# Two ways to form the shift of an exponent, beside a busy GpSimd

## The chip, the cores and the metric

The kernel runs on one core of a Trainium2 chip. The metric is the device time of one execution, in microseconds, and the median over the runs is compared. The core has TensorE (PE, with its weight loads PEld), VectorE (DVE), ScalarE (ACT), GpSimd (POOL) and SyncE (SP), which run their own instruction streams and meet at semaphores.

## The reference, cut to what matters

The work is an attention with random features, then a mixture of experts, then a second feed-forward network. Only the first part is touched:

```python
def phi(x):
    proj = np.einsum('bhsd,md->bhsm', x, omega)
    sq = np.sum(x * x, axis=-1, keepdims=True) / 2.0
    h = proj - sq
    h = h - np.max(h, axis=-1, keepdims=True)
    return np.exp(h) / np.sqrt(m)
q_p, k_p = (phi(q_s), phi(k_s))
kv = np.einsum('bhsm,bhsd->bhmd', k_p, v)
z = np.sum(k_p, axis=2)
num = np.einsum('bhsm,bhmd->bhsd', q_p, kv)
den = np.einsum('bhsm,bhm->bhs', q_p, z)[..., None] + 1e-06
return (num / den).astype(np.float32)
```

There are 4 batches, 8 heads, 576 tokens, 64 values to a head and 128 features. The exponent of a feature is proj + shift, where the shift of a token and head is -|x|²/2 - max h. Here |x|² is the sum of squares and max h is max proj - |x|²/2.

## The kernel before, in words

The 2304 tokens are 18 tiles of 128. A tile of keys (kp) or queries (qp) goes through these stages, each of them a method:

- `load` (L118) brings the tile with its features as rows of the array, and `load_rows` (L133) brings it with tokens on the partitions, both by SP's DMA queue.
- `squares` (L146) squares the tokens in place on GpSimd, a 128x512 product of two SBUF inputs.
- `sums` (L152) adds the squares of each head on VectorE, `ssq` of 128x8 (L157). It then issues the load of the rows two tiles on and the squares of the next tile.
- `colsplit` (L163) rounds the columns on ScalarE, and `colrest` (L173, the instruction at L181) subtracts, which gives the low part, `kpl` or `qpl`. Keys up to tile 6 do this on VectorE, all others on GpSimd.
- `proj` (L185) makes 24 products on TensorE into two PSUM banks, four heads to a bank. Most come from a ring of three banks, `pj`, so the second bank of one projection is free only when the exponentials of the projection before have read theirs.
- `most` (L204) takes the maximum over the features on VectorE, one reduction to a bank (L209), into `mx` of 128x8.
- `shift` (L211) makes `hm` = c·ssq + mx (L216) and `bias` = c·ssq - hm (L220), with c = -SCALE²/2. Both are VectorE operations with two 128x8 inputs in SBUF.
- `expo` (L223) makes eight exponentials on ScalarE, one to a head, with a column of `bias` each (L232).

`attention` (L397) writes the order by hand: one slot per tile, and each engine runs its instructions in the order in which the code issues them. First come five key tiles (L433). Slots 0 to 12 then work on a tile of keys, k = s + 5, and a tile of queries. In such a slot the order is: transposes of the last query features (`t_step`), shift of the last queries, sums of the keys, exponentials of the last queries, `t_rest`, sums of the queries, products of keys and values (`kv`), projection, maximum and shift of the keys, exponentials of the keys, `n_step` (outputs of queries two tiles back, L305, with five small VectorE operations), `x_step`, then projection and maximum of the queries. The shift of those queries comes at the start of the next slot. Slots 13 to 17 have queries alone; there the shift follows its maximum at once (L527).

`beside` (L842) puts work for the next stage between: in slots 8 to 15 GpSimd issues loads of expert weights (L574), in slots 10, 11, 12, 14 and 17 it subtracts a 128x1024 low part of such a weight (`lo_m`, L568), and in slots 14 to 17 a 128x288 part of the tokens (`xl_m`, L642). All these stand in GpSimd's one queue with the squares and the subtractions of `colrest`.

After the slots the two feed-forward networks run, products back to back on TensorE to the end.

The two operations of the shift:

```python
hm = self.qpool.tile([P, H], F32, tag="hm", name=f"hm_{tag}{t}", bufs=3)
nc.vector.scalar_tensor_tensor(hm, ssq, -0.5 * SCALE * SCALE, mx, op0=ALU.mult, op1=ALU.add)
if between:
    between()
bias = self.qpool.tile([P, H], F32, tag="bias", name=f"bias_{tag}{t}", bufs=3)
nc.vector.scalar_tensor_tensor(bias, ssq, -0.5 * SCALE * SCALE, hm, op0=ALU.mult, op1=ALU.subtract)
```

Of the kernel before, what the change touches and what calls it, by code (L numbers as in the profile page):

```python
# [7 lines left out]
F32 = mybir.dt.float32  # L8
# [29 lines left out]
def pieces(t):  # L38
    """(batch, first partition, last partition) of the tokens in tile t"""
    out, p = [], 0  # L40
    while p < P:
        b = (t * P + p) // S
        q = min(P, (b + 1) * S - t * P)
        out.append((b, p, q))
        p = q
    return out


class Kern:
# [5 lines left out]

# [1 line left out]
    def setup(self):  # L57
# [23 lines left out]

# [1 line left out]
    def bank(self, tag, name):  # L83
# [5 lines left out]
    def setup_attn(self):  # L89
        nc = self.nc  # L90
        self.cols, self.rows, self.vin, self.pj, self.bias = {}, {}, {}, {}, {}
        self.kv_ps = {}
        self.kp, self.qp, self.qpT, self.kv, self.xr = {}, {}, {}, {}, {}
        self.gpool = self.qpool
        self.lg = self.qpool.tile([P, NT, E], F32, name="lg")
        self.hl, self.ssq, self.mx = {}, {}, {}
        w = self.qpool.tile([P, 2 * M], F32, name="wom")
        nc.sync.dma_start(out=w, in_=self.a["wom"])
        nc.vector.tensor_scalar(w, w, SCALE, None, op0=ALU.mult)
        self.womh = self.qpool.tile([P, 2 * M], F32R, name="womh")  # L100
        self.woml = self.qpool.tile([P, 2 * M], F32R, name="woml")
        nc.vector.tensor_copy(self.womh, w)
        nc.vector.tensor_tensor(self.woml, w, self.womh.bitcast(F32), ALU.subtract)

    def gate_weights(self, wg):
        """two heads' at a time: block-diagonal w_gate"""
        nc = self.nc
        for j in range(2):
            nc.vector.tensor_copy(self.wg[j * D : (j + 1) * D, :, j, :], wg[j * D : (j + 1) * D])

    def warm(self):
        """products of no use, until the first tokens are here: the array's clock rises with use"""
        x = self.oneh.rearrange("p t e -> p (t e)")[:, 0:P]
        ps = self.bank("w0", "warm")
        for i in range(8):
            self.nc.tensor.matmul(ps[:, 0:P], x, x, start=True, stop=True)

    def load(self, tag, t):  # L118
        """one tile's tokens as columns, for the projection"""
        if t >= NT:  # L120
            return
        pool = self.kpool if tag == "kp" else self.qpool
        x = pool.tile([P, DM], F32, tag=tag + "c", name=f"{tag}c{t}", bufs=3 if tag == "kp" else 2)
        self.nc.sync.dma_start(out=x, in_=self.a["kk" if tag == "kp" else "qq"][t, :, 0, :])
        self.cols[tag, t] = x
# [26 lines left out]
    def sums(self, tag, t):  # L152
        if t >= NT:
            return
        sq = self.rows.pop((tag, t))
        ssq = self.ssq[tag, t] = self.qpool.tile([P, H], F32, tag="ssq", name=f"ssq_{tag}{t}", bufs=5)
        self.nc.vector.tensor_reduce(ssq, sq.rearrange("p (h d) -> p h d", h=H), axis=AX.X, op=ALU.add)  # L157
        if tag == "qp" or t > 5:
            self.load_rows(tag, t + 2)
        if tag == "qp" and t < 13 or tag == "kp" and t > 4:  # L160
            self.squares(tag, t + 1)
# [23 lines left out]
    def proj(self, tag, t):  # L185
        """two heads at a time: block-diagonal omega"""
        nc = self.nc
# [16 lines left out]
    def most(self, tag, t):  # L204
        """max over the features of x . omega"""
        mx = self.mx[tag, t] = self.qpool.tile([P, H], F32, tag="mx", name=f"mx_{tag}{t}", bufs=3)
        for i, ps in enumerate(self.pj[tag, t]):
            out = mx[:, 4 * i : 4 * i + 4]
            self.nc.vector.tensor_reduce(out, ps.rearrange("p (h m) -> p h m", h=4), axis=AX.X, op=ALU.max)  # L209

    def shift(self, tag, t, between=None):  # L211
        """- |x|^2 / 2 - max h, h = x . omega - |x|^2 / 2"""
        nc = self.nc
        ssq, mx = self.ssq.pop((tag, t)), self.mx.pop((tag, t))
        hm = self.qpool.tile([P, H], F32, tag="hm", name=f"hm_{tag}{t}", bufs=3)
        nc.vector.scalar_tensor_tensor(hm, ssq, -0.5 * SCALE * SCALE, mx, op0=ALU.mult, op1=ALU.add)  # L216
        if between:
            between()
        bias = self.qpool.tile([P, H], F32, tag="bias", name=f"bias_{tag}{t}", bufs=3)
        nc.vector.scalar_tensor_tensor(bias, ssq, -0.5 * SCALE * SCALE, hm, op0=ALU.mult, op1=ALU.subtract)  # L220
        self.bias[tag, t] = bias

    def expo(self, tag, t):  # L223
        """exp(h - max h)"""
        nc = self.nc
# [11 lines left out]
    def kv_part(self, b, t, i):  # L237
        """k'^T [v 1] of one tile and four heads, added to batch b's; the bank's first product clears the bank's flags"""
        nc = self.nc
# [22 lines left out]
    def kvg_turn(self, b):  # L262
        """k'^T v with its features first"""
        nc = self.nc
# [7 lines left out]
    def kvg(self, b):  # L272
        """k'^T v w_gate, head by head"""
        nc = self.nc
# [30 lines left out]
    def n_step(self, t):  # L305
        """tokens' outputs and the gate's logits, which are sums over the heads"""
        nc = self.nc
# [34 lines left out]

# [1 line left out]
    def gating(self, t0, t1):  # L344
# [16 lines left out]
    def gates(self, t0, t1):  # L361
        """the gate of a token's expert is 1 / sum of the exponentials; squared, as a later layer needs it"""
        nc = self.nc
# [9 lines left out]
    def counting(self, b):  # L373
        """tokens of each expert"""
        nc = self.nc
# [7 lines left out]
    def counted(self, b):  # L383
        """the fullest expert, and how many tokens are elsewhere"""
        nc, g, cn = self.nc, self.gpool, self.cnt[:, b, :]
# [11 lines left out]
    def attention(self, beside):  # L397
        """one slot per tile of tokens; every stage works on the tile one slot behind the stage before it"""
        nc = self.nc
        ends = {0: 0, 4: 1, 9: 2, 13: 3}  # L400

        def kv(s):
            """products of slot s: a tile's, and what the tile before has of the next batch"""
            t = s + 4
            for i in range(2):
                for tt, bb in [(t - 1, 1), (t, 0)]:
                    if 0 <= tt < NT and bb < len(pieces(tt)):
                        self.kv_part(pieces(tt)[bb][0], tt, i)
            if s in ends:
                self.kv_close(ends[s])  # L410
# [125 lines left out]
    def all_counted(self):  # L536
        """how many tokens of all are not with their batch's expert; what the general path reads"""
        nc = self.nc
# [4 lines left out]

# [1 line left out]
    def stage(self, name):  # L545
        return self.stg.tile([P, 2 * DM], F32, tag="st", name=name, bufs=4)

    def routed(self, b):
        """register with the expert that most tokens of batch b have"""
        self.expert[b] = self.nc.values_load(  # L550
# [7 lines left out]
    def split(self, pool, f, st, name, engines):  # L558
        """hi: 12 significant bits, lo: the rest; hi + lo is the float32 value"""
        nc = self.nc  # L560
# [31 lines left out]
    def narrow_load(self, c):  # L592
        """half a chunk of the FFN's float64 weights, as pairs of words"""
        f, i = divmod(c, 2)
# [4 lines left out]
    def narrow(self, c):  # L599
        """float64 -> float32: sign and top exponent bit, then 7 + 20 bits of the high word, then 3 of the low"""  # L600
        nc = self.nc
# [12 lines left out]

# [1 line left out]
    def steps(self):  # L616
# [10 lines left out]
    def xsplit(self, key, c):  # L627
        """hi and lo of 128 features of one half batch (or block)"""
        nc = self.nc
# [29 lines left out]
    def hidden(self, st):  # L659
        """relu (for the second FFN squared), hi and lo"""  # L660
        nc = self.nc
# [58 lines left out]
    def ffn_next(self):  # L720
        """first layer of the step after this one"""
        nxt = self.todo[self.at + 1] if self.at + 1 < len(self.todo) else None
# [15 lines left out]
    def extras(self, s):  # L738
        """weights made ready beside step s"""
        ev = self.events.get(s, [])  # L740
# [28 lines left out]

# [1 line left out]
    def general(self):  # L771
        """every expert over every token, masked, and the second FFN again; float32 products"""
        nc, tc = self.nc, self.tc
# [169 lines left out]
```

## Time and profile before

| what | us |
|---|---|
| median of 3 runs | 807.91 |
| the three runs | 807.91, 809.21, 801.22 |
| span of the profiled execution | 800.9 |

The page of the profile does not list a run time of the profiled execution beside its span. The span is what the trace covers from the first to the last instruction; it stands 0.3 us below the shortest of the runs and 7.0 us below their median.

How to read the rows further on: a row of a group of instructions ends with the time it was busy, the mean of one in ns, the idle time of its engine just before, and what ended that idle time. A row of a line (L157 and so on) gives the shortest, the median and the longest. A row of a timeline begins with the start and the length in us. [...]

### The profile page before, as it was taken

The numbers are of one execution on the slowest core, as the hardware profiler recorded it, in microseconds if no ns is written. First come the engines' busy times: TensorE is split into PE (matmuls) and PEld (weight loads), VectorE is DVE, ScalarE is ACT, GpSimd is POOL, SyncE is SP. The second block draws the span as 40 slices with busy tenths as digits, with TensorE's granted clock in tenths as the row PEclk, the third lists the DMA queues.
The fourth block names the chain that finished last, engine by engine and source line by source line (L and its number), as shares of the span: only waits on it lengthen the run. The fifth ranks groups of instructions, "written<-read, shape, count | busy, mean of one in ns | idle before, by whom it ended". The sixth has DMA issues, their size and how long they took to land.

```text
span 800.9 us, 12830 instructions
## 1 busy us (share of the span) xinstructions
PE 779.3 (97%) x4944; PEld 732.7 (91%) x4944; DVE 456.1 (57%) x900; ACT 332.7 (42%) x786; POOL 108.4 (14%) x114
## 2 busy tenths in 40 slices
PE   8999989889999999999999999999999999999997
PEld 7999978889999999999999999999999999999986
DVE  7888988896787788887874322322332232232222
ACT  4768657675433444334444322332232223233222
POOL 3546545561101001000000000000000000000000
PEclk9899989899999999999999999999999999999999
DMA  8746553362575666666660010010010001001001
GB/s 277 232 133 191 180 162 113 122 185 80 190 244 181 209 207 223 196 198 202 219 222 6 1 40 0 1 41 1 0 40 1 1 1 40 1 1 40 0 1 43
DMA packets 41603, 84.57 MB, mean 106 GB/s; under 512 B 4000, under 2 KB 13360, under 8 KB 41536
## 3 DMA queue, kind: packets, MB, share of 16 engines
q1 hardware_dynamic: 36864, 66.82, 25.6%
q0 software_dynamic: 4672, 16.86, 6.7%
q8 instruction: 41, 0.67, 0.3%
q14 instruction: 26, 0.21, 0.1%
HBM read 65.76 MB, written 17.91 MB: 104 GB/s over the span
## 4 chain that ended last, share of the span: by engine, by line
PE 86%; DVE 9%; ACT 1%; DMA 1%; issue 1%; POOL 0%; SPq 0%; ACTq 0%; POOLq 0%; DVEq 0%
PE y_f L702 25%; PE h_f L656 8%; PE h_f L655 8%; PE h_f L654 8%; PE y_m L692 4%; PE h_m L654 4%; PE h_m L655 4%; PE y_m L693 4%; PE y_m L694 4%; PE h_m L656 4%; PE n_ps L316 2%; PE kv_ps L245 2%; DVE bias_qp L220 2%; DVE mx_qp L209 1%; DVE hm_qp L216 1%; DVE mx_kp L209 1%
## 5 line engine op out<-in xcount | busy, mean ns | idle before, releaser
L675 DVE TENSOR_TENSOR r_f<-r_f,h_f 128x384 f32<-128x384 f32 x96 | 53.2, 554 | 255.1 <-ACT hh_f L674 255.1
L673 ACT ACTIVATE r_f<-h_f 128x384 f32<-128x384 f32 x96 | 47.1, 491 | 264.7 <-PE h_f L656 264.7
L702 PE MATMUL y_f<-hi_f,hh_f 128*128 128x512 f32 x288 | 113.6, 394 | 0.0
L702 PE MATMUL y_f<-lo_f,hh_f 128*128 128x512 f32 x288 | 113.5, 394 | 0.0
L702 PE MATMUL y_f<-hi_f,hl_f 128*128 128x512 f32 x288 | 113.3, 393 | 0.0
L669 ACT ACTIVATE hh_m<-h_m 128x288 fp32r<-128x288 f32 x64 | 26.4, 412 | 119.6 <-PE h_m L656 118.4
L654 PE MATMUL h_m<-xh_m,hi_m 128*128 128x288 f32 x256 | 75.8, 296 | 0.0
L692 PE MATMUL y_m<-hh_m,hi_m 128*128 128x288 f32 x256 | 75.6, 295 | 0.0
L655 PE MATMUL h_m<-xl_m,hi_m 128*128 128x288 f32 x256 | 75.4, 295 | 0.0
L694 PE MATMUL y_m<-hh_m,lo_m 128*128 128x288 f32 x256 | 75.4, 294 | 0.0
L693 PE MATMUL y_m<-hl_m,hi_m 128*128 128x288 f32 x256 | 75.4, 294 | 0.0
L656 PE MATMUL h_m<-xh_m,lo_m 128*128 128x288 f32 x256 | 75.4, 294 | 0.0
L702 PEld LDWEIGHTS y_f<-hi_f,hl_f 128*128 128x128 f32 x288 | 54.1, 188 | 12.4
L656 PE MATMUL h_f<-xh_f,lo_f 128*128 128x384 f32 x192 | 64.8, 337 | 0.0
L656 PE MATMUL h_f<-x_f,lo_f 128*128 128x384 f32 x192 | 64.8, 337 | 0.0
L655 PE MATMUL h_f<-xl_f,hi_f 128*128 128x384 f32 x192 | 64.7, 337 | 0.0
L655 PE MATMUL h_f<-x_f,hi_f 128*128 128x384 f32 x192 | 64.7, 337 | 0.0
L654 PE MATMUL h_f<-xh_f,hi_f 128*128 128x384 f32 x192 | 64.7, 337 | 0.0
L654 PE MATMUL h_f<-x_f,hi_f 128*128 128x384 f32 x192 | 64.6, 337 | 0.0
L702 PEld LDWEIGHTS y_f<-lo_f,hh_f 128*128 128x128 f32 x288 | 54.2, 188 | 8.8
L702 PEld LDWEIGHTS y_f<-hi_f,hh_f 128*128 128x128 f32 x288 | 54.0, 188 | 8.4
L676 DVE TENSOR_TENSOR hl_f<-r_f,hh_f 128x384 fp32r<-128x384 f32 x96 | 53.6, 559 | 10.4 <-PE y_f L702 0.5
(131 smaller groups left out, 1718.8 us busy)
## 6 DMA issues: line engine op xcount, KB each, us to landing
we<-we POOLq DMA_DIRECT2D x32, 512.0 KB, 5.1
wd<-wf SPq DMA_DIRECT2D x32, 512.0 KB, 5.3
wscr<-narrow SPq DMA_DIRECT2D x32, 256.0 KB, 2.1
wf<-wscr SPq DMA_DIRECT2D x16, 512.0 KB, 4.4
vin<-vv SPq DMA_DIRECT2D x18, 260.0 KB, 3.9
kpc<-kk SPq DMA_DIRECT2D x18, 256.0 KB, 3.5
kpr<-kk SPq DMA_DIRECT2D x18, 256.0 KB, 3.7
qpc<-qq SPq DMA_DIRECT2D x18, 256.0 KB, 3.0
```

The lines of the kernel that those rows point to most:

```text
L209: self.nc.vector.tensor_reduce(out, ps.rearrange("p (h m) -> p h m", h=4), axis=AX.X, op=ALU.max)
L654: nc.tensor.matmul(ps[:, :n], w1, xh[:, :n], start=(c == 0), stop=False)
L655: nc.tensor.matmul(ps[:, :n], w1, xl[:, :n], start=False, stop=False)
L656: nc.tensor.matmul(ps[:, :n], w2, xh[:, :n], start=False, stop=(c == KC - 1))
L669: nc.scalar.activation(hh[:, :n], ps, AF.Relu)
L673: nc.scalar.activation(r, ps, AF.Relu)
L675: nc.vector.tensor_tensor(r, r, ps, ALU.mult)
L676: nc.vector.tensor_tensor(hl, r, hh.bitcast(F32), ALU.subtract)
L692: nc.tensor.matmul(out, w1, hh[:, :HALF], start=(f == 0), stop=False)
L693: nc.tensor.matmul(out, w1, hl[:, :HALF], start=False, stop=False)
L694: nc.tensor.matmul(out, w2, hh[:, :HALF], start=False, stop=last)
L702: nc.tensor.matmul(acc[i], h[:, i * P : (i + 1) * P], w[:, DM:], start=(f == 0 and k == 0), stop=(last and k == 2))
```

## The change

The two-input operations of `shift` go. In their place a tile `three` of 128x8x3 holds, for each token and head, the maximum, -|x|²/2, and -max h. The first column is written by `most` itself. The second is written in `sums` by a new GpSimd operation, which scales `ssq` by c. `shift` then makes two reductions on VectorE: the negated sum of columns 0 and 1 into column 2, and the sum of columns 1 and 2 into `bias`. `ssq` has three buffers in place of five, and `three` has five. The argument `between`, which no caller used, goes too, and docstrings and comment lines are emptied, which makes no instruction.

```diff
     def sums(self, tag, t):
...
         sq = self.rows.pop((tag, t))
-        ssq = self.ssq[tag, t] = self.qpool.tile([P, H], F32, tag="ssq", name=f"ssq_{tag}{t}", bufs=5)
+        ssq = self.qpool.tile([P, H, 1], F32, tag="ssq", name=f"ssq_{tag}{t}", bufs=3)
         self.nc.vector.tensor_reduce(ssq, sq.rearrange("p (h d) -> p h d", h=H), axis=AX.X, op=ALU.add)
+        three = self.three[tag, t] = self.qpool.tile([P, H, 3], F32, tag="three", name=f"three_{tag}{t}", bufs=5)
+        self.nc.gpsimd.tensor_scalar(three[:, :, 1:2], ssq, -0.5 * SCALE * SCALE, None, op0=ALU.mult)
         if tag == "qp" or t > 5:
             self.load_rows(tag, t + 2)
         if tag == "qp" and t < 13 or tag == "kp" and t > 4:
...
     def most(self, tag, t):
-        """max over the features of x . omega"""
-        mx = self.mx[tag, t] = self.qpool.tile([P, H], F32, tag="mx", name=f"mx_{tag}{t}", bufs=3)
+
+        three = self.three[tag, t]
         for i, ps in enumerate(self.pj[tag, t]):
-            out = mx[:, 4 * i : 4 * i + 4]
+            out = three[:, 4 * i : 4 * i + 4, 0:1]
             self.nc.vector.tensor_reduce(out, ps.rearrange("p (h m) -> p h m", h=4), axis=AX.X, op=ALU.max)
 
-    def shift(self, tag, t, between=None):
-        """- |x|^2 / 2 - max h, h = x . omega - |x|^2 / 2"""
-        nc = self.nc
-        ssq, mx = self.ssq.pop((tag, t)), self.mx.pop((tag, t))
-        hm = self.qpool.tile([P, H], F32, tag="hm", name=f"hm_{tag}{t}", bufs=3)
-        nc.vector.scalar_tensor_tensor(hm, ssq, -0.5 * SCALE * SCALE, mx, op0=ALU.mult, op1=ALU.add)
-        if between:
-            between()
+    def shift(self, tag, t):
+
+        nc = self.nc
+        three = self.three.pop((tag, t))
+        nc.vector.tensor_reduce(three[:, :, 2:3], three[:, :, 0:2], axis=AX.X, op=ALU.add, negate=True)
         bias = self.qpool.tile([P, H], F32, tag="bias", name=f"bias_{tag}{t}", bufs=3)
-        nc.vector.scalar_tensor_tensor(bias, ssq, -0.5 * SCALE * SCALE, hm, op0=ALU.mult, op1=ALU.subtract)
+        nc.vector.tensor_reduce(bias, three[:, :, 1:3], axis=AX.X, op=ALU.add)
         self.bias[tag, t] = bias
```

## Rows read from the trace of the kernel before

**Rows 1.** The page: span, busy time of TensorE, and its granted clock in 40 slices.
```profile
span 800.9 us, 12830 instructions
...
PE 779.3 (97%) x4944; PEld 732.7 (91%) x4944; DVE 456.1 (57%) x900; ACT 332.7 (42%) x786; POOL 108.4 (14%) x114
...
PEclk9899989899999999999999999999999999999999
```

**Rows 2.** Windows by stretch: busy time of each engine, granted clock, DMA share, GB/s.
```profile
8.00:42.00 34.00, 32.89 (x228) 31.17 (x228) 30.46 (x57) 23.11 (x77) 18.11 (x16) 0.90 0.78 263
108.00:118.00 10.00, 9.28 (x52) 9.12 (x53) 8.12 (x18) 6.56 (x21) 3.50 (x4) 0.66 0.39 120
142.00:152.00 10.00, 8.31 (x45) 8.31 (x46) 7.27 (x22) 6.40 (x19) 3.36 (x5) 0.66 0.32 102
196.00:800.00 604.00, 599.12 (x3505) 560.39 (x3502) 292.38 (x541) 202.66 (x396) 13.82 (x26) 1.00 0.26 85
...
42.00:183.00 141.00, 128.10 (x1079) 122.63 (x1079) 123.32 (x265) 98.00 (x300) 73.95 (x66) 0.95 0.50 154
```

**Rows 3.** Waits in 42 to 183 us: who for whom, total, times, longest.
```profile
ACT qp L232 <- DVE bias_qp L220: 14.2, 7, 3.6
PE pj_kp L200 <- ACT qp L232: 7.0, 5, 2.6
PE pj_qp L200 <- ACT qp L232: 2.9, 3, 1.1
```

**Rows 4.** Timeline of 103 to 108 us, a slot with a long shift.
```profile
103.40 1.26 POOL L181 TENSOR_TENSOR qpl<-qpc,qph 128x512 fp32r<-128x512 f32 x1 [3.56 <-ACT qph L170]
103.62 1.07 DVE L216 SCALAR_TENSOR_TENSOR hm_qp<-ssq_qp,mx_qp 128x8 f32<-128x8 f32 x1
...
104.72 2.71 DVE L220 SCALAR_TENSOR_TENSOR bias_qp<-ssq_qp,hm_qp 128x8 f32<-128x8 f32 x1
...
105.35 1.05 POOL L150 TENSOR_TENSOR kpr<-kpr 128x512 f32<-128x512 f32 x1
...
106.36 1.04 POOL L150 TENSOR_TENSOR qpr<-qpr 128x512 f32<-128x512 f32 x1
...
107.52 0.62 ACT L232 ACTIVATE qp<-pj_qp,bias_qp 128x128 f32<-128x128 f32 x2 [3.55 <-DVE bias_qp L220]
```

**Rows 5.** Groups of 0 to 330 us: the four groups of the shift.
```profile
L220 DVE SCALAR_TENSOR_TENSOR bias_qp<-ssq_qp,hm_qp 128x8 f32<-128x8 f32 x18 | 16.4, 911 | 0.8
...
L216 DVE SCALAR_TENSOR_TENSOR hm_kp<-ssq_kp,mx_kp 128x8 f32<-128x8 f32 x18 | 10.9, 605 | 0.6
L216 DVE SCALAR_TENSOR_TENSOR hm_qp<-ssq_qp,mx_qp 128x8 f32<-128x8 f32 x18 | 10.7, 597 | 0.6
...
L220 DVE SCALAR_TENSOR_TENSOR bias_kp<-ssq_kp,hm_kp 128x8 f32<-128x8 f32 x18 | 4.8, 264 | 0.7
```

**Rows 6.** Lines L220, L157 and L350: shortest, median and longest in ns.
```profile
L220 DVE SCALAR_TENSOR_TENSOR bias_kp<-ssq_kp,hm_kp x18: 166/168/1117, 12.3 to 146.2; 128x8 f32<-128x8 f32 x18
...
L157 DVE TENSOR_REDUCE ssq_qp<-qpr x18: 669/675/678, 28.6 to 178.8; 128x8 f32<-128x512 f32 x18
...
L350 DVE TENSOR_REDUCE gmx<-lg x4: 177/184/188, 89.9 to 198.7; 128x5 f32<-128x40 f32 x2, 128x4 f32<-128x32 f32 x2
```

**Rows 7.** Window of 106 to 108 us, of the two-microsecond windows.
```profile
106.00:108.00 2.00, 0.13 (x2) 0.00 (x0) 2.00 (x3) 0.48 (x2) 1.40 (x2) 1.00 0.95 305
```

**Rows 8.** Groups on GpSimd, the first three in 42 to 183 us, the last over the span.
```profile
L568 POOL TENSOR_TENSOR lo_m<-we,hi_m 128x1024 fp32r<-128x1024 f32 x5 | 11.9, 2378 | 0.1
...
L574 POOL DMA_DIRECT2D we<-we x8 | 4.9, 607 | 0.0
L642 POOL TENSOR_TENSOR xl_m<-xT,xh_m 128x288 fp32r<-128x288 f32 x4 | 3.2, 790 | 2.4 <-ACT xh_m L640 2.4
...
L935 POOL MEMSET const-float32-0.0<- 128x1 f32 x1 | 0.1, 98 | 0.5 <-issue 0.5
```

**Rows 9.** Timeline of the start, 2 to 40 us: squares of key tile 1, shift of tile 0.
```profile
9.77 1.04 POOL L150 TENSOR_TENSOR kpr<-kpr 128x512 f32<-128x512 f32 x1 [2.65 <-DMA kpr<-kk]
...
11.28 1.00 DVE L216 SCALAR_TENSOR_TENSOR hm_kp<-ssq_kp,mx_kp 128x8 f32<-128x8 f32 x1
```

More of the change, by code (lines that the diff above doesn't have):

```diff
@@ L95, in setup_attn @@
         self.lg = self.qpool.tile([P, NT, E], F32, name="lg")
-        self.hl, self.ssq, self.mx = {}, {}, {}
+        self.hl, self.three = {}, {}
         w = self.qpool.tile([P, 2 * M], F32, name="wom")
```

## The prediction

> **What bounds the kernel now.** I read the page first. By its busy time TensorE works 97% of the 800.9 us, and its granted clock falls under 9 tenths in several of the first slices [rows 1]. So an average says little, and the second view is the windows by stretch. From 196 us to the end TensorE is busy 599.1 of 604 us at full clock with VectorE at 292.4, so nothing that VectorE saves there can count [rows 2]. The slots of the attention, 42 to 183 us, are another matter. Of these 141 us TensorE is idle for 141 - 128.1 = 12.9, and VectorE is busy for 123.3. [...]
>
> Third, the waits: in the slots TensorE stands for 7.0 us at the keys' projection and 2.9 us at the queries', both until the queries' exponentials have read a bank of the ring, and those exponentials stood 14.2 us for `bias` [rows 3]. So the chain there is: maximum, shift, exponentials, second bank of the next projection. Fourth, the timeline of one slot shows what the shift is made of. `hm` begins while GpSimd makes `qpl` and ends at 104.69, 0.03 us after `qpl` does at 104.66. `bias` ends at 107.43, 0.03 us after GpSimd's squares at 107.40. Two operations on 8 columns took 1.07 and 2.71 us, and ScalarE stood 3.55 us for them [rows 4]. The shortest `bias` took 0.166 us [rows 6]. So a two-input VectorE operation waits from inside for the GpSimd work beside it, to its end. In the window of 106 to 108 us TensorE is busy 0.13 of 2 us [rows 7], and the stretch that follows is the first of the two at 0.66 [rows 2].
>
> **What is removed.** 36 `hm` and 36 `bias`, 16.4 + 10.9 + 10.7 + 4.8 = 42.8 us of VectorE [rows 5]. At 0.166 each they would be 72 x 0.166 = 12.0 [rows 6]. The other 30.8 us are waiting.
>
> **What is added on VectorE.** 72 reductions of 16 values to 8. Does a reduction wait for GpSimd? The 18 of `ssq_qp` lie between 669 and 678 ns, and they too run beside squares and subtractions, so I say no; if it did, nothing would be saved (third rival). Their size: 512 values take 675 ns and 32 to 40 take 184, so (675 - 184)/(512 - 36) = 1.03 ns a value, and 16 values give 0.163 us [rows 6]. Below that they can't fall far, and above 0.184 they should not rise, as the larger ones take that. I take 0.17, or 12.2 us. VectorE saves 42.8 - 12.2 = 30.6 us. The maxima write with a stride of three words in place of one; I count that at nothing, with 0.1 us each as the bound, an estimate.
>
> [...] Were a small one as dear as the 512-value ones, 72 x 0.675 = 48.6 us would replace 42.8, and the time would be no better than before; the row of L350 shows that size sets the price [rows 6].
>
> **What is added on GpSimd.** 36 scalings of 8 columns. No such operation stands in the trace. From below it is a 128x1 fill, 0.098 us, from above the subtraction of 288 columns, 0.79 us [rows 8]. I take 0.2, nearer to the fill because the work is 8 columns: 7 us in all. GpSimd is busy 74.0 of the 141 us [rows 2], so the cover is 67 us, and even at 0.79 (28 us) it would hold in sum. What counts is where it stands. In `sums` it is issued ahead of the next squares and of all that GpSimd does after it: the squares, `kpl`, `qpl` and the loads of expert weights. So the squares now wait for VectorE's sum, which they did not. They are wanted a slot later, so that costs nothing unless a slot shrinks to GpSimd's own work. The load of the rows, issued by SP, stays where it was, and SP is not held, since GpSimd alone issues the scaling. `ssq` with three buffers is read by the scaling soon after; I see no wait there.
>
> **The new wait.** The shift waits for the scaling, and behind it on VectorE stand `bias`, the operations of `n_step` and the next maxima, and ScalarE's exponentials and TensorE's second bank wait for those. Whether the maxima, which write other columns of the same tile, wait too I can't see in this trace; if so the wait comes some 1.3 us earlier, as two maxima stand between. In most slots GpSimd finishes `qpl` (1.26 us) before or while VectorE sums the keys, then scales, and two more sums or copies and two maxima cover that. In slots 10, 11, 12, 14 and 17 `lo_m` (2.38 us) and an issue of a load (0.61 us) come between [rows 8]; there I expect up to 1 us of wait each, 5 us in all, and the bound from below is none. At the start the scaling of tile 0 stands behind the squares of tile 1, which end at 10.81, before `hm` began at 11.28 [rows 9], so nothing is lost if only the shift waits, and about 1 us if the maxima do.
>
> **The sum.** Not all of 30.6 us is on the path, because TensorE becomes the bound. It can win back its idle time, 12.9 us. I take three quarters, 9.7, and leave the rest to the slots with `lo_m` and to the latency of the chain. It can also win back the low clock: in each of the two stretches (1 - 0.66) x 10 = 3.4 us, so 6.8, as the idle time ahead of them goes. The low clock near the start, (1 - 0.90) x 34 = 3.4 us, I leave in, since little changes before it [rows 2]. So 9.7 + 6.8 = 16.5 us, and 800.9 - 16.5 = 784.4 by the profiled execution. That one lies 7.0 us under the median of the runs, 807.9. What the runs had more may be stalls and low clock of the same kind, which go, or something else, which stays. I take half: 784.4 + 3.5 = **788 us**.
>
> [...]
>
> **Rivals.** One: *TensorE is the bound already.* Half of its idle time goes, 6.5 us, and the low clock comes back after other gaps. That gives 800.9 - 6.5 = 794.4, and 798 with the same 3.5. For it speaks that TensorE is busy 128.1 of 141 us [rows 2]; against it that its waits are named, and 9.9 us of them hang on the queries' exponentials [rows 3].
>
> Two, on the other side: *GpSimd's queue sets the pace.* The maxima wait for the scaling, and the scaling for `qpl` or `lo_m`. Then the old wait stays in another place, and the two maxima, which ran before it, now run after it: some 1.36 us for each of the 18 key tiles, 24.5 us of VectorE. With about half on the path, as 16.5 of 30.6 above, that is +13, so 821 us. It decides from the point where the scaling ends more than 30.6/36 = 0.85 us, on the mean of all tiles, after the first maximum could start. For it speaks that GpSimd runs `qpl` just as the shift begins [rows 4], against it its 67 idle microseconds.
>
> Three: *the change doesn't do what it says.* The small reductions are held by GpSimd as the old operations were; then only the scalings are added, 809 us. Against it stand the even times of the sums [rows 6].
>
> **Chances.** Forecast 0.68, rival one 0.20, two 0.05, three 0.07. A difference of 1%, 8 us, is about what a measurement of this kernel can tell from no change; under 799.8 is faster. The forecast gives 0.66 faster and 0.02 same, rival one 0.14 and 0.06, rival three 0.06 same and 0.01 slower, rival two 0.05 slower: 0.80, 0.14, 0.06. The range: if all of TensorE's idle time and all three stretches of low clock go, 12.9 + 10.2 = 23.1 gives 777.8, and the gaps of the weight loads or all 30.6 us lie a little lower; I put 776. Upward it takes in rival one with 4 us to spare, 802.
>
> **What would show it.** Right: the 72 reductions lie near 0.17 us with no long one; ScalarE's wait for `bias` falls from 14.2 to under 4 us; no TensorE gap of over 2 us in the slots; the granted clock from 108 us on stays at 1.00; the first network begins some 16 us earlier and the rest is as long as before. Wrong: VectorE or ScalarE waits for GpSimd's scaling for more than 10 us in sum, TensorE's waits for the exponentials stay, or small reductions take over 0.5 us.

## The result, and the profile after

The changed kernel takes 780.8 us (median of four runs, 776.9 to 781.0) where the kernel before takes 804.9 on the same chip (median of four, 801.2 to 809.2): a ratio of 0.969, with a 95% interval of 0.9645 to 0.9736. That is 24.1 us less. The forecast was 788 from a median of 807.9, so 19.9 less; the median of before is 804.9 now because a fourth run took 801.8.

The page after: span, busy times, granted clock, and the line that opens the chain of work that ended last.

```profile
span 779.2 us, 12902 instructions
...
PE 767.3 (98%) x4944; PEld 723.4 (93%) x4944; DVE 429.4 (55%) x900; ACT 332.7 (43%) x786; POOL 118.3 (15%) x150
...
PEclk9999999999999999999999999999999999999999
...
PE 95%; DVE 2%; DMA 1%; ACT 0%; SPq 0%; issue 0%; POOL 0%; DVEq 0%
```

Against [rows 1] the span falls by 21.7 us and VectorE by 26.7, and GpSimd gains 9.9. In the chain VectorE is now 2%; it was 9% before, with TensorE at 86%.

Where did the 21.7 go? I cut both traces at two products that both have: the key-value product behind the transpose of the keys of the slots (41.61 us before, 38.20 after) and the first product of the first network (181.85 and 160.56). The rest of the span is as long as it was, 619.0 and 618.6 us. So 3.4 us were gained ahead of the slots, 17.9 in them and 0.4 behind. The slots of before by this cut, in the view of [rows 2]:

```profile
41.61:181.85 140.24, 127.34 (x1075) 121.87 (x1073) 122.59 (x263) 97.08 (x296) 73.19 (x66) 0.95 0.50 155
```

And after, with a stretch of low clock and the two networks:

```profile
38.20:160.56 122.36, 119.60 (x1075) 116.52 (x1073) 100.38 (x264) 97.21 (x296) 81.60 (x94) 0.99 0.56 177
...
108.00:112.00 4.00, 4.00 (x24) 4.00 (x22) 1.64 (x4) 0.00 (x0) 2.23 (x2) 0.57 0.67 243
...
175.00:779.00 604.00, 598.81 (x3502) 560.08 (x3500) 292.04 (x541) 202.75 (x396) 13.85 (x26) 1.00 0.26 85
```

Read the first number (the length) less the second (TensorE busy): 12.9 us idle before, 2.8 after, so 10.1 won. The clock (the third figure from the end, a fraction of full speed): the two stretches of 10 us at 0.66 in [rows 2] lost 3.4 each, so 6.8 before; after, the stretch of 4 us at 0.57 loses 1.7, so about 5.1 won. These make 15.2 of the 17.9. Read the third number, the weight loads, in place of the second and the gaps are 18.4 before and 5.8 after, 12.5 won, and 12.5 + 5.1 = 17.6. The records of the products overlap: from 105.38 to 105.85 us of before they start 0.12 us apart and are listed with 0.28 each, where the weight loads are listed with 0.19. So a gap of up to 0.16 us between two products would not show, and of up to 0.07 between two weight loads.

The groups that answer to [rows 5], with the scalings that are new:

```profile
L159 POOL TENSOR_SCALAR three_kp<-ssq_kp 128x8 f32<-128x8 f32 x18 | 5.7, 316 | 8.0 <-DVE ssq_kp L157 7.0
L159 POOL TENSOR_SCALAR three_qp<-ssq_qp 128x8 f32<-128x8 f32 x18 | 4.2, 234 | 2.8 <-DVE ssq_qp L157 1.4
...
L219 DVE TENSOR_REDUCE bias_kp<-three_kp 128x8 f32<-128x16 f32 x18 | 3.1, 170 | 0.7
L219 DVE TENSOR_REDUCE bias_qp<-three_qp 128x8 f32<-128x16 f32 x18 | 3.1, 170 | 0.8
...
L217 DVE TENSOR_REDUCE three_kp<-three_kp 128x8 f32<-128x16 f32 x18 | 3.1, 170 | 2.0
L217 DVE TENSOR_REDUCE three_qp<-three_qp 128x8 f32<-128x16 f32 x18 | 3.1, 170 | 1.8
```

Four times 3.1 is 12.4 us in place of 42.8, with no long one: the longest of these 72 takes 0.172. The slot that answers to [rows 4] shows why that helps:

```profile
95.86 1.27 POOL L183 TENSOR_TENSOR qpl<-qpc,qph 128x512 fp32r<-128x512 f32 x1 [2.80 <-ACT qph L172]
...
96.46 0.17 DVE L217 TENSOR_REDUCE three_qp<-three_qp 128x8 f32<-128x16 f32 x1
...
96.67 0.17 DVE L219 TENSOR_REDUCE bias_qp<-three_qp 128x8 f32<-128x16 f32 x1
...
96.93 2.18 ACT L231 ACTIVATE qp<-pj_qp,bias_qp 128x128 f32<-128x128 f32 x8 [0.19 <-DVE bias_qp L219]
```

Both reductions run while GpSimd makes `qpl`, which ends at 97.13; before, `hm` ended 0.03 us behind that subtraction and `bias` 0.03 us behind the squares. That slot was no exception: of the 72 operations of before, 31 take over 0.25 us, and each of the 31 ends 0.02 to 0.03 us behind an instruction of GpSimd. What they take above 0.168 us each comes to 30.7 us, which is all of the waiting. ScalarE stood 0.19 us for `bias` here, and 3.55 there. The waits of 42 to 165 us:

```profile
ACT kp L231 <- DVE bias_kp L219: 12.9, 7, 4.8
...
PE t_ps L295 <- DVE lgh L326: 2.5, 2, 1.6
...
ACT qp L231 <- DVE bias_qp L219: 1.5, 5, 0.7
...
PEld pj_qp L202 <- ACT kp L231: 0.4, 2, 0.2
...
PEld pj_qp L202 <- ACT qp L231: 0.2, 1, 0.2
```

And two lines of the waits of before, 42 to 183 us, beside those of [rows 3]:

```profile
ACT kp L232 <- DVE bias_kp L220: 5.5, 3, 2.1
...
PE pj_qp L200 <- ACT kp L232: 2.1, 4, 0.7
```

ScalarE's wait for the queries' `bias` has gone from 14.2 to 1.5, but its wait for the keys' has risen from 5.5 to 12.9, so the sum fell only from 19.7 to 14.4. What counts is what reaches TensorE. Its products stood 9.9 us for the queries' exponentials and 2.1 for the keys'; none of these waits is left at its products, and 0.2 and 0.4 at its weight loads.

### The profile page after: what moved, and what is told of

It is laid out like the page before. It is cut to its first block, busy times and chain, and to the rows that moved or that the text cites. A ratio compares the mean times of both kernels' runs of the same rounds, so it can differ in the third digit from the quotient of the medians.

```text
span 779.2 us, 12902 instructions
## 1 busy us (share of the span) xinstructions
PE 767.3 (98%) x4944; PEld 723.4 (93%) x4944; DVE 429.4 (55%) x900; ACT 332.7 (43%) x786; POOL 118.3 (15%) x150
## 4 chain that ended last, share of the span: by engine, by line
PE 95%; DVE 2%; DMA 1%; ACT 0%; SPq 0%; issue 0%; POOL 0%; DVEq 0%
PE y_f L701 26%; PE h_f L655 9%; PE h_f L654 9%; PE h_f L653 9%; PE kv_ps L244 5%; PE y_m L691 4%; PE h_m L653 4%; PE h_m L654 4%; PE y_m L693 4%; PE y_m L692 4%; PE h_m L655 4%; PE n_ps L315 3%; PE t_ps L295 2%; PE pj_qp L202 1%; PE pj_kp L202 1%; PE pj_qp L203 1%
## 5 line engine op out<-in xcount | busy, mean ns | idle before, releaser
L701 PEld LDWEIGHTS y_f<-hi_f,hl_f 128*128 128x128 f32 x288 | 54.1, 188 | 12.4
```

Source lines behind the costliest of these rows:

```text
L701: nc.tensor.matmul(acc[i], h[:, i * P : (i + 1) * P], w[:, DM:], start=(f == 0 and k == 0), stop=(last and k == 2))
```

## The experiments

Each ratio is against the kernel before on the same chip, whose medians were 801.5 to 802.5. My theory: a VectorE operation that reads two tiles of SBUF waits from inside for GpSimd's work beside it and a reduction doesn't, and this wait, not the count or size of the operations, is what the change took away.

**The same tile, but two-input operations.**

```diff
-nc.vector.tensor_reduce(three[:, :, 2:3], three[:, :, 0:2], axis=AX.X, op=ALU.add, negate=True)
+nc.vector.tensor_tensor(three[:, :, 2], three[:, :, 0], three[:, :, 1], ALU.add)
-nc.vector.tensor_reduce(bias, three[:, :, 1:3], axis=AX.X, op=ALU.add)
+nc.vector.tensor_tensor(bias, three[:, :, 1], three[:, :, 2], ALU.subtract)
```

> The changed kernel with everything kept (tile of three columns, scaling on GpSimd, three buffers of ssq), but the two reductions of the shift made again by two-input operations on the same columns. Theory (waiting): a VectorE operation with two SBUF inputs waits for the GpSimd operation beside it, a reduction does not, and this is all of the gain. Then the time goes back near that of before, 800 us (794 to 806), and the two operations take over 0.5 us in the mean. Rival (layout): the gain comes from the scaling being off VectorE, the tile of three or the buffers. Then the time stays at 781 us (778 to 784) and the operations at 0.17 us.

Measured: 801.9 us, ratio 1.000 (0.997 to 1.003). The groups, same stretch as [rows 5]:

```profile
L217 DVE TENSOR_TENSOR three_qp<-three_qp 128x8 f32<-128x8 f32 x18 | 12.7, 707 | 1.8
L219 DVE TENSOR_TENSOR bias_qp<-three_qp 128x8 f32<-128x8 f32 x18 | 11.0, 610 | 0.8
L219 DVE TENSOR_TENSOR bias_kp<-three_kp 128x8 f32<-128x8 f32 x18 | 9.9, 551 | 0.7
...
L217 DVE TENSOR_TENSOR three_kp<-three_kp 128x8 f32<-128x8 f32 x18 | 6.1, 340 | 3.0 <-POOL three_kp L159 1.3
```

They sum to 39.7 us where before has 42.8, and the whole gain is gone, with the scaling on GpSimd, the tile of three columns and the order of the change all kept. The kind of operation is the cause; the rest of the change by itself moves nothing that can be measured.

**Only the second operation two-input.**

```diff
-nc.vector.tensor_reduce(bias, three[:, :, 1:3], axis=AX.X, op=ALU.add)
+nc.vector.tensor_tensor(bias, three[:, :, 1], three[:, :, 2], ALU.add)
```

> The changed kernel with only the second operation of the shift made by two inputs, the first stays a reduction. Theory (waiting): the second now stands where the first stood and waits for the same GpSimd work, so nearly all of the waiting comes back in one operation: its mean is over 0.9 us, time 796 us (789 to 802). Rival (each operation pays its own wait): about half of the loss, mean of the second near 0.6 us, time 787 to 791.

Measured: 789.4 us, ratio 0.986 (0.980 to 0.991).

```profile
L219 DVE TENSOR_TENSOR bias_qp<-three_qp 128x8 f32<-128x8 f32 x18 | 14.1, 783 | 0.8
L219 DVE TENSOR_TENSOR bias_kp<-three_kp 128x8 f32<-128x8 f32 x18 | 6.8, 380 | 0.7
```

The time lies in both ranges, so the means decide. I had thought that the second operation would take over the wait that the first no longer makes, with over 0.9 us in the mean, and that theory falls: it takes 0.58, and in sum 14.1 + 6.8 = 20.9 us, as with both two-input, 11.0 + 9.9 = 20.9. That the two sums are equal is partly chance, as the queries pay 3.1 us more and the keys 3.1 less. The rival held: each operation pays for what GpSimd runs beside it, and each that is replaced gives its own share back, here some 12 us of the 21 to 24 of the whole change.

**Before, without the squares.** The squares on GpSimd are left out, so the sums add the values themselves; half of the sum cancels in the exponent.

```diff
 def squares(self, tag, t):
...
-        self.nc.gpsimd.tensor_tensor(x, x, x, ALU.mult)
+        pass
```

> The kernel before without the squares on GpSimd: its sums add the tokens' values and not their squares. Theory (waiting): bias of the queries waited mostly for the squares, so its mean of 911 ns falls under 350 ns, while hm, which waits for the subtractions of colrest and of the expert weights, keeps 450 to 700 ns; time 790 us (784 to 797). Rival (the long operations come from their own semaphores or from VectorE): means as before and time within 3 us of before.

Measured: 794.2 us, ratio 0.991 (0.989 to 0.994).

```profile
L216 DVE SCALAR_TENSOR_TENSOR hm_qp<-ssq_qp,mx_qp 128x8 f32<-128x8 f32 x18 | 13.5, 749 | 0.6
L216 DVE SCALAR_TENSOR_TENSOR hm_kp<-ssq_kp,mx_kp 128x8 f32<-128x8 f32 x18 | 8.6, 478 | 0.6
L220 DVE SCALAR_TENSOR_TENSOR bias_qp<-ssq_qp,hm_qp 128x8 f32<-128x8 f32 x18 | 7.2, 398 | 0.8
...
L220 DVE SCALAR_TENSOR_TENSOR bias_kp<-ssq_kp,hm_kp 128x8 f32<-128x8 f32 x18 | 3.0, 167 | 0.7
```

This is the same cause from the other side: with VectorE's code untouched, less work on GpSimd makes `bias` of the queries fall from 911 to 398 ns. I expected under 350 there and 790 us. The time came 7.6 us under the 801.8 of before. What stayed is `hm` of the queries, which rose from 597 to 749, above what I expected: `qpl` and the low parts of the weights still run beside it, and all 21 operations that still take over 0.25 us end 0.02 to 0.03 us behind `kpl`, `qpl` or a low part. The squares carry 42.8 - 32.3 = 10.5 us of the waiting, a third.

**Scaling on VectorE.** Does an operation with one input wait too?

```diff
-self.nc.gpsimd.tensor_scalar(three[:, :, 1:2], ssq, -0.5 * SCALE * SCALE, None, op0=ALU.mult)
+self.nc.vector.tensor_scalar(three[:, :, 1:2], ssq, -0.5 * SCALE * SCALE, None, op0=ALU.mult)
```

> The changed kernel with the scaling of the sums on VectorE instead of GpSimd; it has one input, of 8 columns in SBUF. Theory (only two SBUF inputs wait): the 36 scalings take some 0.17 us each, 6 us of VectorE that has room, and the time stays at 781 us (777 to 784). Rival (any VectorE operation of this kind may wait for GpSimd): their mean is over 0.4 us, and the time 786 to 795 us.

Measured: 785.4 us, ratio 0.982 (0.973 to 0.991). The groups, and one slot's timeline:

```profile
L159 DVE TENSOR_SCALAR three_qp<-ssq_qp 128x8 f32<-128x8 f32 x18 | 11.0, 613 | 0.6
...
L159 DVE TENSOR_SCALAR three_kp<-ssq_kp 128x8 f32<-128x8 f32 x18 | 8.6, 476 | 0.6
```

```profile
56.43 1.27 POOL L183 TENSOR_TENSOR qpl<-qpc,qph 128x512 fp32r<-128x512 f32 x1 [3.55 <-ACT qph L172]
...
57.12 0.61 DVE L159 TENSOR_SCALAR three_kp<-ssq_kp 128x8 f32<-128x8 f32 x1
...
58.66 1.04 POOL L150 TENSOR_TENSOR qpr<-qpr 128x512 f32<-128x512 f32 x1
...
58.95 0.78 DVE L159 TENSOR_SCALAR three_qp<-ssq_qp 128x8 f32<-128x8 f32 x1
```

The time lies between the two ranges, and the means, 0.61 and 0.48 us, are the rival's. My theory in its narrow form ("only two inputs wait") falls. The scaling ends at 57.73, 0.03 us behind `qpl` at 57.70, and at 59.73, 0.03 behind the squares at 59.70. Its shortest takes 0.172 us, its longest 2.640; 36 x 0.172 = 6.2 of the 19.6 us are work. Of the three kinds tried here only the reductions stay at their size, 0.170 us in the mean and 0.172 at the longest. So the scaling's place on GpSimd is a part of the gain, by the medians some 5 of the 21 to 24 us; the intervals of the ratios overlap, so that size is rough. Why the reductions don't wait no run shows.

**The scaling later.** It is put behind the next tile's squares and a product of no use on GpSimd, to find what the new wait costs.

```diff
-        self.nc.gpsimd.tensor_scalar(three[:, :, 1:2], ssq, -0.5 * SCALE * SCALE, None, op0=ALU.mult)
...
             self.squares(tag, t + 1)
+        junk = self.qpool.tile([P, 320], F32, tag="junk", name=f"junk_{tag}{t}", bufs=1)
+        self.nc.gpsimd.tensor_tensor(junk, sq[:, 0:320], sq[:, 0:320], ALU.mult)
+        self.nc.gpsimd.tensor_scalar(three[:, :, 1:2], ssq, -0.5 * SCALE * SCALE, None, op0=ALU.mult)
```

> The changed kernel with the scaling put behind the squares of the next tile on GpSimd, and behind a product of 320 columns into a tile that nothing reads: the scaling comes some 1.9 us later, and GpSimd has 28 us more work. In the profile of the changed kernel the scaling of a key tile ends 2.6 us ahead of the shift that reads it (56.19 and 58.82 us in one slot). Theory (GpSimd's queue has that much to spare): 781 to 785 us, VectorE's wait for the scaling under 6 us in sum. Rival (GpSimd's queue is the next limit): the waits come to over 15 us and the time to 788 us or more.

Measured: 784.1 us, ratio 0.977 (0.970 to 0.983).

```profile
DVE three_kp L219 <- POOL three_kp L165: 4.8, 4, 1.7
...
DVE three_qp L219 <- POOL three_qp L165: 1.7, 3, 0.7
```

Delayed by some 1.8 us a tile (the squares' 1.04 and 0.75 of the product), the scaling holds VectorE for 6.5 us in seven places, a little over the 6 that I expected at most, and the run takes 3 us more, in which the product's own weight on GpSimd is not told apart. The waiting line is the shift (L219 here), never the maxima (L213), though these write columns of the same tile. That answers what the prediction left open, and with it goes its second rival.

**Only the maxima.** The half square stands in h and in max h, and cancels. So the rows' loads, squares, sums, scalings and both reductions are left out, and the maximum is written with its sign turned, as `bias`.

```diff
-            out = three[:, 4 * i : 4 * i + 4, 0:1]
-            self.nc.vector.tensor_reduce(out, ps.rearrange("p (h m) -> p h m", h=4), axis=AX.X, op=ALU.max)
+            out = bias[:, 4 * i : 4 * i + 4]
+            self.nc.vector.tensor_reduce(out, ps.rearrange("p (h m) -> p h m", h=4), axis=AX.X, op=ALU.max, negate=True)
```

> The changed kernel with bias taken as the negated maximum alone (the half square cancels in exact arithmetic): the rows' loads, squares, sums, scalings and the two small reductions are left out, some 36 us of VectorE and 48 us of GpSimd. Theory (after the change TensorE is the bound in the slots): little is left to win, its 2.8 us of gaps and some of the start: 773 us (769 to 778). Rival (VectorE or GpSimd still sets the pace): half of VectorE's 36 us comes off, 763 us or less.

Measured: 770.8 us, ratio 0.962 (0.956 to 0.967). The slots of its profiled run, and two stretches of low clock:

```profile
36.00:153.00 117.00, 117.00 (x1039) 115.30 (x1038) 72.52 (x177) 94.82 (x291) 47.57 (x40) 0.96 0.43 132
...
30.00:36.00 6.00, 6.00 (x41) 5.93 (x39) 1.56 (x3) 2.40 (x8) 1.65 (x2) 0.72 0.43 132
...
102.00:114.00 12.00, 12.00 (x65) 11.93 (x65) 4.07 (x9) 5.10 (x13) 2.70 (x3) 0.57 0.18 61
```

The profiled run is the slowest of the five, 776.9 us; the other four take 769.8 to 771.7, with a mean clock of 0.995 to 0.998 where this one has 0.989, so they can't hold all of this low clock. TensorE is never idle in the slots, while VectorE is busy 72.5 of 117 us, against 100.4 of 122.4 in the changed kernel. So without any shift TensorE is the bound there, and all that leads to the shift costs the changed kernel 7 to 10 us still (it takes 24.1 us less than before on its chip, this run 31.1 less on its own). And the clock falls here with TensorE busy all of the time.

**Full rows.** Those stretches begin inside runs of 32 products over 64 of the 128 rows, for the two tiles which two batches share. Here these products run over all 128 (the sums then hold the other batch's tokens too).

```diff
-                self.kp[t][lo:hi, 4 * i + j, :],
-                self.vin[t][lo:hi, 4 * i + j, :],
+                self.kp[t][:, 4 * i + j, :],
+                self.vin[t][:, 4 * i + j, :],
```

> The changed kernel with the products of keys and values of the two tiles that two batches share made over all 128 rows instead of 64 (the other batch's tokens are added too). The number of products and their columns stay. Theory (the low clock that is left comes with the 64-row products, since both stretches begin inside or right behind a run of them, with TensorE busy): the granted clock stays at 1.00 from 20 us on, and the time falls by the 3 to 4 us of the two stretches, 777 us (774 to 779). Rival (it comes from something else): both stretches stay, 781 us.

Measured: 777.3 us, ratio 0.969 (0.962 to 0.975). Stretches of the changed kernel, then the same ones here:

```profile
26.00:38.00 12.00, 12.00 (x86) 11.45 (x86) 7.70 (x19) 8.51 (x30) 9.02 (x12) 0.86 0.64 204
...
100.00:116.00 16.00, 16.00 (x124) 15.63 (x124) 10.09 (x27) 10.41 (x32) 8.07 (x10) 0.89 0.52 177
```

```profile
26.00:38.00 12.00, 11.49 (x102) 11.29 (x102) 9.71 (x23) 10.39 (x35) 10.01 (x14) 1.00 0.62 216
100.00:116.00 16.00, 15.90 (x141) 15.70 (x141) 11.40 (x28) 12.96 (x39) 9.80 (x11) 1.00 0.51 169
```

Both low stretches are gone, and 3.5 us with them. Three of its four runs have a mean clock of 0.998, one 0.994. But that the 64 rows are the cause isn't shown. The run with only the second operation two-input makes the 64-row products as the changed kernel does (32 of them from 30.19 and from 106.87 us), and its clock stays up:

```profile
30.00:40.00 10.00, 9.74 (x83) 9.19 (x81) 7.75 (x17) 9.32 (x32) 7.73 (x10) 1.00 0.60 193
108.00:116.00 8.00, 8.00 (x69) 7.86 (x70) 4.36 (x12) 4.36 (x17) 4.75 (x7) 1.00 0.60 190
```

Nine kept traces have two such runs of 32 each, and a low stretch begins inside ten of the 18; of the four runs over full rows, two here and two in the next kernel, none has one. And the changed kernel's own fastest execution, 776.9 us at a mean clock of 0.998, is as fast as the fastest here. So 3.5 us is what the low clock costs; what brings it is suggested only.

**Both together.** Only the maxima, and for the shared tiles a value tile with zeros at the other batch's tokens, so that products over 128 rows give the same sums.

```diff
+        if len(pieces(t)) > 1:
+            for b, lo, hi in pieces(t):
+                v = self.vin[t, b] = self.kpool.tile([P, H, VW], F32, tag=f"vs{lo}", name=f"vin{t}_{b}", bufs=1)
+                rest = slice(hi, P) if lo == 0 else slice(0, lo)
+                self.nc.gpsimd.memset(v[rest], 0.0)
+                self.nc.sync.dma_start(out=v[lo:hi], in_=self.a["vv"][t][lo:hi])
+            return
...
-                self.kp[t][lo:hi, 4 * i + j, :],
-                self.vin[t][lo:hi, 4 * i + j, :],
+                self.kp[t][:, 4 * i + j, :],
+                self.vin[t, b][:, 4 * i + j, :],
```

> Two findings together: bias is the negated maximum alone, as in the run with only the maximum, and the products of the two shared tiles run over 128 rows, with the other batch's tokens of the value tile filled with zeros. In the slots of the run with only the maximum TensorE has no gaps, and what is left is two stretches of low clock, 2 to 3 us and 5 us. Theory (the low clock comes with the 64-row products): both go, 766 us (763 to 769). Rival: they stay or come elsewhere, 771 us.

Measured: 768.8 us (768.5 to 768.9), ratio 0.959 (0.956 to 0.963), with a mean clock of 0.998 or 0.999 in each run. It beats both kernels, by 4.1% and by 1.5%, and lies at the upper end of the range.

```profile
36.00:151.00 115.00, 115.00 (x1069) 113.93 (x1069) 75.70 (x184) 97.25 (x294) 51.83 (x44) 1.00 0.45 137
```

**The changed kernel once more**, beside it on the same chip.

> The changed kernel as it is, on the same chip as the run before it, for the distance between the two: 781 us (777 to 784), with or without one of the two stretches of low clock, by which its runs differ by about 4 us.

Measured: 780.4 us, ratio 0.973 (0.969 to 0.977): the first result again. One stretch of its profiled run:

```profile
122.00:136.00 14.00, 12.46 (x88) 12.09 (x87) 10.04 (x31) 8.74 (x25) 6.64 (x8) 0.76 0.29 94
```

Here the low clock follows 1.5 us in which TensorE stood idle, and 108 to 112 us, right behind its 64-row products, is at 1.00. So the clock falls behind idle time too, and not at these products in every run.

## Why the prediction was right, and where its terms were not

- **The cause and the saving on VectorE**: right. 30.4 us saved, 30.6 worked out; 170 ns a reduction, as taken; a maximum takes 0.683 to 0.688 us after and took 0.683 to 0.684 before, so its new stride costs nothing. The two-input and squares runs show the cause from both engines. Nor is a small reduction as dear as one of 512 values, the case in which the prediction saw no gain: 0.170 us stands beside the 0.166 of the shortest `bias` [rows 6].
- **The scalings**: 0.2 us taken, 0.316 (keys) and 0.234 (queries) measured, 9.9 us for 7. They lie beside other work and cost nothing that shows.
- **The new wait**: up to 5 us expected in five slots, none measured; it comes only when the scaling is delayed by some 1.8 us.
- **ScalarE's wait**: the sign "under 4 us" holds for the queries' `bias`, 1.5, and not with the keys', 14.4 in sum. The prediction counted the queries' alone. Two other signs held: the longest gap of TensorE in the slots is 1.64 us, and the first network begins 21.3 us earlier.
- **TensorE's idle time**: the step was too small. Three quarters of 12.9 gave 9.7; 10.1 went by that measure and 12.5 by the weight loads. With the second figure the account of the slots closes to 0.3 us. The gaps of the weight loads, which the range names, were 141 - 122.6 = 18.4 us [rows 2]. With three quarters of them, 13.8, the sum would have been 780.3 for a span of 779.2, in place of 784.4; that it comes so near is luck, as the start, which neither sum has, makes up for 13.8 and 6.8 being too large.
- **The low clock**: 6.8 expected back, about 5.1 came. The step "as the idle time ahead of them goes" holds for 142 to 152 us in the first profile; in the repeat a stretch came back behind idle time. At 108 us TensorE was busy throughout and the clock fell all the same: the sign "at 1.00 from 108 us on" was wrong. It fell at the end of the 64-row products, and that these are the cause is not shown.
- **The start**: the largest miss. Nothing expected, 3.4 us measured. At 7.3 us a projection product of before took 0.41 us, one of after 0.28, but the lead is lost again as TensorE then stands 1.45 us for `kpl` of VectorE: the first product that reads tile 1's `kpl` starts at 11.41 before and 11.21 after. By 28 us the lead is 1.9. VectorE, for which the products wait there, has lost 0.8 at `hm` of tile 0 (1.00 us for 0.17, [rows 9]) and 0.8 at a copy of the gate's weights which stood beside squares (two copies in 1.21 us, in 0.36 after). The last 1.5 us is a shorter stretch of low clock, (33.61 x 0.10) - (30.20 x 0.06).
- **The 3.5 us added to the median**: wrong. The runs of after lie within 4.1 us of each other, those of before within 8.0. Of the 7.0 us between span and median 1.7 was no difference between executions at all: each run whose span is listed stands 1.5 to 2.0 us above it, so after with 780.9 for 779.2. What the slower runs of before had more went too.
- **The rivals**: TensorE as the bound is near where the change ends, not where it began; GpSimd's queue and held reductions are excluded by the waits and the groups above.

## What to carry to other kernels

Where a VectorE operation of a few columns takes anything from its floor to several times that, compare its end with the ends of GpSimd's instructions: 0.02 to 0.03 us behind one of them, as with 31 of the 72 operations here, is a wait that no view lists. Here a reduction over a small tile took it off, with 0.170 us in the mean for 0.264 to 0.911, and so did the scaling's place on the other engine, with 0.316 and 0.234 us for 0.476 and 0.613. Then cut both traces at the same two instructions and count TensorE's gaps by its weight loads as well as by its products.

## What was not expected of the hardware

The wait goes both ways. At the start four of GpSimd's scalings meet a subtraction of VectorE that came first and take 0.56 to 0.65 us in place of 0.23, as this one, which ends 0.14 behind that subtraction at 15.13:

```profile
14.45 0.68 DVE L183 TENSOR_TENSOR kpl<-kpc,kph 128x512 fp32r<-128x512 f32 x1
...
14.62 0.65 POOL L159 TENSOR_SCALAR three_kp<-ssq_kp 128x8 f32<-128x8 f32 x1 [0.80 <-DVE ssq_kp L157]
```

And it moves on to what is left. VectorE's busy time fell by 26.7 us and not by 30.4, since other two-input operations now meet GpSimd more than before: of the gating, `gsh` takes 1.6 us more in sum and `gfi` 1.0, and `kpl` on VectorE 1.4. Here `gfi`, on 32 columns, meets `kpl` and takes 1.22 us, where it took 0.19; TensorE's longest gap in the slots, 1.64 us, lies behind it, at the transposes:

```profile
122.40 1.29 POOL L183 TENSOR_TENSOR kpl<-kpc,kph 128x512 fp32r<-128x512 f32 x1
122.52 1.22 DVE L355 SCALAR_TENSOR_TENSOR gfi<-gsh,rank 128x32 f32<-128x32 f32 x1
```

Of the clock it stays open why it fell at the 64-row products in some executions and not in others. Why the first products of before took 0.41 us each, while the windows list 1.00 there, has a plainer answer: the trace's record of the clock begins at 10.75 us in before and at 5.76 in after, and it is there that the products turn to 0.28 us. Ahead of the first entry the listed 1.00 is no reading; 0.41 us is what the same products of after take from 108.33 to 110.46 us, and from 109 to 111 us the windows list 0.50.
